# Moving a filter's second transform into the first stage and reordering the borders between batch pairs, in a long convolution followed by spectral mixing

## The chip, the core and the metric

The kernel runs on one core of one Trainium2 chip. The metric is the device time of one execution in microseconds, the median of several runs. A core has five engines with an instruction queue each: TensorE (PE, with its weight loads PEld), VectorE (DVE), ScalarE (ACT), GpSimd (POOL) and SyncE (SP). DMAs are issued here from the queues of SP and POOL. Engines meet through semaphores. Matmuls write to PSUM, of which there are eight banks; DVE and ACT read PSUM and write to SBUF ("evict").

## The reference

Two operators in a row, on `x` of 8 x 5696 x 128 (batch, sequence, channel):

```python
# 1: a causal convolution along the sequence by a filter h of 5696 x 128
L = 2 * S
Xf = np.fft.rfft(x, n=L, axis=1)
Hf = np.fft.rfft(h, n=L, axis=0)
x = np.fft.irfft(Xf * Hf[None, :, :], n=L, axis=1)[:, :S, :]
# 2: mixing of the lowest 64 modes with complex 128 x 128 weights
X = np.fft.rfft(x, axis=1)
Xr, Xi = np.real(X[:, :64]), np.imag(X[:, :64])
Y = np.zeros_like(X)
Y[:, :64] = (Xr @ w_r - Xi @ w_i) + 1j * (Xr @ w_i + Xi @ w_r)   # per mode
u = x + np.fft.irfft(Y, n=S, axis=1)
out = u + np.maximum(u @ w_ch, 0.0)
```

## The kernel before, in words

Each Fourier transform is a chain of matmuls with constant tables. A recorder (`R.add`) takes every operation in program order, adds the waits that its reads and writes need, and emits one instruction stream for each engine. So the order of the calls is the order on each engine, and most instructions of the profile carry the line of a small helper: L320 for every matmul, L308 to L314 for evictions, L317 for DMAs.

The sequence is cut as 89 x 64, and 90 frequencies `k` stand for the long axis (`NK`). They are handled in 23 groups, called ticks, of up to four frequencies (`NT = 23`, `KT = 4`; the last has two). The batch is handled in four pairs (`NP = 4`).

- **First transform**, `a_tile(j, slots, eng)` (L438), for j from 0 to 31: four matmuls of the input tile `Xin` with the table `F` into a slot of two PSUM banks, and one eviction of 128 x 720 into `As`. For j = 31 the eviction is halved: DVE takes the first bank and ACT the second ("both"). For the first pair the slots go round (0, 2, 4, 6), and `share(n)` (L428) gives an eviction to the engine with the lower load in a small table of costs, `COST`: 670 on ACT and 815 on DVE for 720 columns, 480 and 600 for 512.
- **The filter** has the same first transform earlier, which leaves `Ah`. Its second transform is `filter_tick(t, banks, eng)` (L455): 16 small matmuls of `Ah` with the table `M`, an eviction of 128 x 512 into `Hs`, two DMAs on SP's queue that copy half of the partitions to the other half, and for six of the ticks a DMA on SP's queue that loads a piece of the table `G` over the part of `Ah` that is no longer needed. `M` arrives in six pieces from POOL's queue. Six filter ticks run among the a_tiles of the first pair; the other 17 run inside the ticks of pair 0, each at the end of `tick`, six ticks ahead of its use (`LH = 6`), and DVE evicts them.
- **A tick** of a pair, `tick(g_, t)` (L612): `second(g_, t)` is the second transform (16 matmuls on `As` and `M`), `products(g_, t)` multiplies it by the filter `Hs` on DVE into `U` (usually ACT first copies PSUM into `Xs`; in a `straight` tick DVE reads PSUM itself). Two ticks later (`LC`) comes the third transform: four matmuls of `U` with `Wc`, two ACT evictions into a buffer `Zs` or `Zt`, and a DMA on SP's queue that stores it to a scratch tensor in DRAM. Three ticks later (`LM`) the matmuls with `G` add up the 64 modes in PSUM bank 7. In pairs 1 to 3 every odd tick is a `twin`: the second transform of the next tick follows in the same run of matmuls; and every fourth product is `straight`. In pair 0 there is no twin and no straight product. Pair 0 starts with six Z buffers, pairs 1 and 2 use ten.
- During a pair's ticks, the input of the next pair is loaded (POOL's queue) and placed into `Xin` by DVE copies (`x_place`).
- **The border** between two pairs: the last ticks have no second transform left, and the a_tiles of the next pair begin. Six of them stand in a table, `border`, inside the last four ticks; the 26 others follow in a loop (L696) whose slots go round (4, 6, 0, 2) after tile 6 and whose evictions alternate ACT and DVE in a fixed pattern of nine. Between the two, ACT evicts bank 7 into `XT`. After tile 31, `keep(8, 6)` issues eight matmuls that compute nothing, into banks 6 and 7. `keep` matmuls also follow the first stage (12) and the first two ticks of pair 0 (8 each). In the loop every odd tile also triggers one copy of a piece of the mixing weights on POOL's queue.
- After the four pairs come the mixing, the inverse transform of the sum and the last product (L705 to L859), which the change does not touch.

Of the kernel before, what the change touches and what calls it, by code (L numbers as in the profile page):

```python
# [123 lines left out]
def bass_long_conv_fft__then__afno_spectral_mix_kernel(nc, x, h, moe_w_r, moe_w_i, moe_w_ch, out):  # L124
# [8 lines left out]
    NP = B // 2  # L133
    KT = 4
    NT = (NK + KT - 1) // KT
# [15 lines left out]
    c, s = np.cos(th), np.sin(th)  # L151
# [75 lines left out]
    g_sb = at("G", GW, F16, a_g)  # L227
    ah_sb = at("Ah", HW, F16, a_g)
    NU, NXS, NZ, NZX = 3, 2, 6, 10
    NZS = [NZ] + [NZX] * (NP - 2) + [8]  # L230
    NZL = NZS[-1]
    a_st = take((2 * NU + NXS + NZ) * 2048)
    h_in = at("Hin", J * D, F16, a_st)
# [3 lines left out]
    XC = 4  # L237
# [214 lines left out]
             [bank(t), bank(t + 1)], [("as", j)], 1.0 / 64, eng=eng, after=once(("hp", j), HP))  # L452


    def filter_tick(t, banks, eng="vector"):  # L455
        n = len(ticks[t])
        hb = banks
        for i, k in enumerate(ticks[t]):
            for r in range(2):
                for dh in range(2):  # L460
                    mm(pv(hb[dh], i * DH, [[1, DH]]),
                       ap(m_sb, MW, J * dh, J, k * 3 * J + (J if r == 0 else 0) + dh * J, [[1, P]]),
                       ap(ah_sb, HW, J * dh, J, (2 * k + r) * DH, [[1, DH]]), r == 0, r == 1,
                       AHT + mtok(k) + [("ag", k)], [bank(hb[dh])])
        lo, hi = KT * t * D, (KT * t + n) * D
        old = once("xr", [t_ for r_ in XR for t_ in r_]) if t == 0 else []
        evac(h_sb[:, lo:hi], pv(hb[0], 0, [[DH, n], [512, 2], [1, DH]]), [bank(hb[0]), bank(hb[1])], [("h", t, 0)],
             eng=eng, after=old)
        for p0, p1 in ((0, J), (J, 0)):
            dma("sync", h_sb[p0:p0 + J, HW + lo:HW + hi], h_sb[p1:p1 + J, lo:hi], "s", [("h", t, 0)], [("h", t, 1, p0)])  # L470
        if t % 2 and t // 2 < NG:
            s0, s1 = t // 2 * GP, min(t // 2 * GP + GP, NS)
            dma("sync", g_sb[:, s0 * P:s1 * P], bass.AP(c_g, s0 * P, [[GW, P], [1, (s1 - s0) * P]]), "c", (),
                [("g", t // 2)], after=[("ag", k) for k in range(s0, s1)])
# [43 lines left out]
            [("s4", part, 0)], after=pace + (AST if part else M_ALL[1:4]))  # L518

    V, A = "vector", "scalar"  # L520
    border = {NT - 1: [(0, 0, V)], NT: [(1, 2, V), (2, 0, V)], NT + 1: [(3, 2, A), (4, 0, V)], NT + 2: [(5, 2, V)]}
    early = {0: lambda: load_id(), 1: lambda: load_w(0), 3: lambda: load_w(1), 6: lambda: load_w(2), 8: lambda: load_w(3),
             12: lambda: load_s4(1), 16: lambda: load_s4(0),
             14: lambda: clear_zt(0),
# [13 lines left out]
        for i in range(n):  # L538
            mm(pv(b0 + i % 2, 0, [[1, 2 * NK]]), f1_sb[:, 0:P], f1_sb[:, :], True, True, [("f1",)], [bank(b0 + i % 2)])

    LC, LM, LH = 2, 3, 6
    ZR = 96
    XBANKS = [bank(0), bank(1), bank(2), bank(3)]

    def with_h_at(g_, t):
        return g_ == 0 and t + LH < NT

    onchip = {}

# [5 lines left out]
        return e  # L555

    def twin(g_, t):
        return g_ > 0 and t % 2 == 1

    def straight(g_, t):  # L560
        return g_ > 0 and t % 4 == 3

    def slot_of(g_, t):
        if g_ == 0 or t == 0:
            return XSLOT[(t + 1) % 2 if t and not with_h_at(g_, t) else 0]
        return XSLOT[((t - 1) // 4 + t) % 2]

    def second(g_, t):
# [32 lines left out]
              bk + [("h", t, 0), ("h", t, 1, 0), ("h", t, 1, J)], [("u", i)])  # L601

    Z_OLD = [("ag", k) for k in range(NS, NS + 8 * (NZX - NZ))]
    XPLACE = [9, 10, 12, 15, 16, 18, 20, 22], [9, 10, 13, 14, 17, 18, 20, 22]

    def zroom(g_, s_):
        return (s_ - 2 * NZ) % NZX if g_ == 0 and s_ >= 2 * NZ else s_ % NZS[g_]

    def xtok(n):
        return [("xt", n, p_) for p_ in range(2)]  # L610

    def tick(g_, t):  # L612
        if g_ + 1 < NP:
            for i in range(2 * XC):
                if t == XPLACE[g_ > 0][i]:
                    x_place(i, x_st[i], xtok(i))
        with_h = with_h_at(g_, t)
        if t < NT:
            of_two = t > 0 and twin(g_, t - 1)
            if not of_two and not (g_ == 0 and t > LC):  # L620
                second(g_, t)
            products(g_, t, slot_of(g_, t))
            if twin(g_, t):
                second(g_, t + 1)
                if straight(g_, t):
                    copied(g_, t + 1, slot_of(g_, t + 1))
        drain = list(border[t]) if t in border and g_ + 1 < NP else []
        if drain and t >= NT:
            j, sl, e = drain.pop(0)
            a_tile(j, [sl], e)  # L630
        if g_ + 1 < NP and t % 2 == 0 and 0 < t <= 4 * XC:
            i = t // 2 - 1
            x_load(g_ + 1, i, x_st[i], xtok(i), [("u", t % NU)] + AST)
        if LC <= t < NT + LC:
            s_ = t - LC
            n = len(ticks[s_])
            i, zi = s_ % NU, zroom(g_, s_)
            zb = [turns("z", ZBANK) for b in range(2)]
            for b in range(2):
                for r in range(2):  # L640
                    mm(pv(zb[b], 0, [[1, n * D]]), (W1, W2)[r], u_s[i][:, r * 1024 + b * 512:r * 1024 + b * 512 + n * D],
                       r == 0, r == 1, [("u", i), ("wc",)] + ([("u0", i)] if s_ == 0 and b else []), [bank(zb[b])])
                evac(bass.AP(z_s[zi], b * D, [[1024, P], [2 * D, n], [1, D]]),
                     pv(zb[b], 0, [[D, n], [1, D]]), [bank(zb[b])], [("zs", zi, b)], eng="scalar",
                     after=once(("zx", zi, b), Z_OLD) if zi >= NZ else ())
            zo = (g_ * NK + KT * s_) * P * 256
            dma("sync", bass.AP(zs, zo, [[256, P], [P * 256, n], [1, 256]]),
                bass.AP(z_s[zi], 0, [[1024, P], [256, n], [1, 256]]), "z",
                [("zs", zi, 0), ("zs", zi, 1)], [("zd", g_, s_)])
            if drain and t >= NT:  # L650
                j, sl, e = drain.pop(0)
                a_tile(j, [sl], e)
        if g_ == 0 and LC <= t < NT - 1:
            second(g_, t + 1)
        if LM <= t < NT + LM:
            s_ = t - LM
            zi = zroom(g_, s_)
            for b in range(2):
                for i, k in sorted(enumerate(ticks[s_]), key=lambda q: (s_ > 0 or q[1] != 1, q)):
                    if k % 2:  # L660
                        o, off, n, sl = pv(MB, b * P, [[1, P]]), (k + 1) // 2 * P, P, (k + 1) // 2
                    else:
                        ms, off = even[k]
                        n, sl = 2 * len(ms), 0
                        dims = [[M, 2]] if len(ms) == 1 else [[ms[1] - ms[0], 2], [M, 2]]
                        o = pv(MB, b * P + ms[0], dims)
                    mm(o, z_s[zi][:, i * 256 + b * P:i * 256 + b * P + P], g_sb[:, off:off + n],
                       k == 1 and b == 0, k == NK - 1 and b == 1, [("g", sl // GP), ("zs", zi, b)], [bank(MB)])
        if drain and t < NT + LM - 1:
            j, sl, e = drain.pop(0)  # L670
            a_tile(j, [sl], e)
        if with_h:
            filter_tick(t + LH, [2, 3])

    SLOTS = [0, 2, 4, 6]
    for j in range(32):
        a_tile(j, [turns("s", SLOTS)], "both" if j == 31 else share(720))
        if j >= 11 and j % 3 == 2 and (j - 11) // 3 < LH:
            b_ = turns("s", SLOTS)
            filter_tick((j - 11) // 3, [b_, b_ + 1], share(512))  # L680
    keep(12, turns("s", SLOTS))
    for g_ in range(NP):
        for t in range(NT + LM):
            tick(g_, t)
            if g_ == 0 and t < 2:
                keep(8, 4)
            assert g_ + 1 < NP or not wp
            if g_ == NP - 1 and t in early:
                pace[:] = [("u", min(t, NT - 1) % NU)]
                early[t]()  # L690
        evac(bass.AP(xt, 2 * g_ * XTW + M, [[B * XTW, P], [XTW, 2], [1, P]]), pv(MB, 0, [[P, 2], [1, P]]),
             [bank(MB)], [("xt", g_)], 1.0 / 64, eng="scalar", after=[("ag", k) for k in range(NS + 2 * XN, NK)])
        evac(bass.AP(xt, 2 * g_ * XTW, [[B * XTW, P], [XTW, 2], [1, M]]), pv(MB, M, [[P, 2], [1, M]]),
             [bank(MB)], [("xtn", g_)], -1.0 / 64, eng="vector" if g_ + 1 == NP else "scalar", after=[("ag", k) for k in range(NS + 2 * XN, NK)])
        if g_ + 1 < NP:
            for j in range(6, 32):  # L696
                a_tile(j, [(4, 6, 0, 2)[(j - 7) % 4] if j > 6 else 0], "both" if j == 31 else (A, V)[(j - 6) % 9 % 2])
                if j == 31:
                    keep(8, 6)
                if wp and j % 2 == 1:  # L700
                    dst, src_, ring, tok = wp.pop(0)
                    dma("gpsimd", dst, src_, ring, (), [tok], after=[("as", j)])
# [189 lines left out]
```

## Time and profile before

| what | value |
|---|---|
| median of three runs | 384.91 us (384.59 to 386.44) |
| the profiled execution | 385.34 us, of it 383.2 us span |
| a_tiles of the first pair, with six filter ticks | 27.97 to 42.63 us |
| second(0) of pairs 0, 1, 2, 3 starts at | 43.88, 109.12, 164.28, 219.06 us |
| first border a_tile of pairs 1, 2, 3 | 93.03, 148.18, 202.97 us |
| Hs evictions on DVE | 22 of 128x512, 686 ns each |
| products from Xs / straight from PSUM | 69 at 1219 ns / 15 at 2284 ns (128x2048) |
| As evictions, 128x720 | ACT 64 at 784 ns, DVE 60 at 903 ns |

All times in the views are microseconds from the start of the span unless marked ns. A row of the timeline gives start, duration, engine, line, operation with its output and input tiles, their shape, and a count when several instructions are merged; in brackets stands the idle time of that engine before it, with what ended it. Rows of matmuls overlap, since they are pipelined: two of 180 columns start 0.078 us apart though each row is 0.24 us long.

### The profile page before, as it was taken

What the parts mean: (1) busy time and instruction counts of PE and PEld (TensorE: products, weight loads), DVE (VectorE), ACT (ScalarE), POOL (GpSimd) and SP (SyncE); (2) the same over time, 40 slices, a digit from 0 to 9 for tenths busy, and PEclk for the clock granted to TensorE, in tenths of its full rate; (3) what the DMA queues carried; (4) which work ended last, traced back from release to release, by engine and by line L of the source; (5) the groups of instructions that cost most, each with busy time, mean ns of one, the idle gap of its engine ahead of it and who ended that gap; (6) DMA issues with size and microseconds to landing.
All of it is one profiled execution on the core that took longest, in us unless ns stands there. A gap on an engine that the chain in (4) does not pass through costs nothing.

```text
span 383.2 us, 12588 instructions
## 1 busy us (share of the span) xinstructions
PE 366.0 (96%) x5392; PEld 283.7 (74%) x5392; DVE 310.5 (81%) x348; ACT 302.7 (79%) x488; POOL 82.5 (22%) x133
## 2 busy tenths in 40 slices
PE   7999899999989999989999999999999999999994
PEld 7998756666866666866667866668898988887873
DVE  6969888998888999998998888875447767776876
ACT  1359688898889997989997999995457676776785
POOL 8400022220552320733310411319200000000000
PEclk9999999999999999999999999997999999999999
DMA  7998469999699997999995859999999999999879
GB/s 149 194 283 339 138 125 291 273 244 261 96 138 210 226 249 220 101 133 204 263 257 164 87 167 370 334 327 388 402 402 398 414 405 406 412 405 378 359 279 356
DMA packets 86865, 103.94 MB, mean 271 GB/s; under 512 B 22638, under 2 KB 72430, under 8 KB 83330
## 3 DMA queue, kind: packets, MB, share of 16 engines
q1 hardware_dynamic: 62523, 67.73, 50.5%
q0 software_dynamic: 24288, 35.43, 44.1%
q8 instruction: 42, 0.69, 0.7%
q14 instruction: 12, 0.10, 0.1%
HBM read 70.61 MB, written 51.12 MB: 318 GB/s over the span
## 4 chain that ended last, share of the span: by engine, by line
PE 69%; ACT 10%; DMA 9%; DVE 6%; POOL 2%; issue 2%; SPq 0%; DVEq 0%; POOLq 0%
PE ps L320 69%; ACT As L310 6%; DMA Xr<-in_x_dram 4%; DMA ZT0b<-zscr 4%; POOL Xr L317 2%; DVE As L314 2%; DVE U L592 1%; ACT UT L308 1%; ACT R L826 1%; ACT Zt L308 1%; DVE Xin L356 1%; ACT Xs L308 1%; DVE U L600 1%; DVE O L827 1%; DVE UT L312 0%
## 5 line engine op out<-in xcount | busy, mean ns | idle before, releaser
L600 DVE TENSOR_TENSOR U<-Xs,Hs 128x2048 f16<-128x2048 f16 (+1 forms) x73 | 86.7, 1190 | 12.0 <-ACT Xs L308 10.4
L320 PE MATMUL ps<-U,Wc 128*128 128x512 f16 (+1 forms) x368 | 94.0, 376 | 0.0
L308 ACT CAST Xs<-ps 128x1024 f16<-128x1024 f32 (+1 forms) x77 | 75.0, 979 | 9.0 <-PE ps L320 7.4
L308 ACT CAST Zs<-ps 128x512 f16<-128x512 f32 (+1 forms) x134 | 70.6, 596 | 5.9 <-PE ps L320 5.8
L827 DVE TENSOR_TENSOR O<-ps,R 128x512 f32<-128x512 f32 x81 | 52.6, 686 | 20.5 <-ACT R L826 15.2
L826 ACT ACTIVATE R<-ps 128x512 f32<-128x512 f32 x96 | 51.0, 573 | 14.2 <-PE ps L320 13.7
L314 DVE TENSOR_SCALAR As<-ps 128x720 f16<-128x720 f32 (+1 forms) x64 | 53.2, 880 | 5.1 <-PE ps L320 3.4
L320 PE MATMUL ps<-F,Xin 128*128 128x180 f16 x512 | 52.3, 250 | 2.6 <-DVE Xin L356 1.2
L320 PE MATMUL ps<-As,M 64*128 64x128 f16 x1440 | 50.6, 217 | 4.2 <-DVE U L592 3.0
L320 PEld LDWEIGHTS ps<-As,M 64*128 64x128 f16 x1440 | 40.3, 94 | 17.9 <-issue 8.1
L310 ACT ACTIVATE As<-ps 128x720 f16<-128x720 f32 x68 | 48.0, 768 | 6.4 <-PE ps L320 5.6
L320 PE MATMUL ps<-WI,UT 128*128 128x256 f16 x360 | 52.0, 279 | 0.5 <-DVE O L827 0.4
L320 PEld LDWEIGHTS ps<-F,Xin 128*128 128x128 f16 x512 | 44.5, 155 | 9.5 <-DVE As L314 2.6
L320 PEld LDWEIGHTS ps<-U,Wc 128*128 128x128 f16 x368 | 28.7, 97 | 27.6 <-ACT Zs L308 4.4
L317 POOL DMA_DIRECT2D Xt<-in_x_dram x48 | 26.0, 545 | 104.6 <-PE ps L320 100.2
L308 ACT CAST UT<-ps 128x712 f16<-128x712 f32 x40 | 30.0, 752 | 18.8 <-PE ps L320 17.8
L320 PEld LDWEIGHTS ps<-WI,UT 128*128 128x128 f16 x360 | 39.3, 152 | 4.4 <-issue 2.1
L320 PE MATMUL ps<-IBs,C 128*128 128x356 f16 x128 | 40.1, 323 | 0.6
L320 PEld LDWEIGHTS ps<-G,Zs 128*128 128x128 f16 x524 | 27.4, 96 | 11.7
L600 DVE TENSOR_TENSOR U<-ps,Hs 128x2048 f16<-128x2048 f32 x15 | 34.3, 2284 | 0.0
L320 PE MATMUL ps<-G,Zs 128*128 128x128 f16 (+2 forms) x524 | 32.6, 192 | 0.0
L320 PE MATMUL ps<-F 128*128 128x180 f16 x280 | 27.7, 254 | 2.5 <-DMA F<-cF 2.5
(86 smaller groups left out, 506.1 us busy)
## 6 DMA issues: line engine op xcount, KB each, us to landing
out_dram<-O SPq DMA_DIRECT2D x39, 512.0 KB, 11.4
zscr<-Zs SPq DMA_DIRECT2D x64, 256.0 KB, 6.8
Xt<-in_x_dram POOLq DMA_DIRECT2D x24, 320.0 KB, 7.0
zscr<-Zt SPq DMA_DIRECT2D x24, 256.0 KB, 6.6
W<-wscr POOLq DMA_DIRECT2D x4, 1024.0 KB, 8.9
M<-cM POOLq DMA_DIRECT2D x5, 720.0 KB, 20.5
ZT0a<-zscr SPq DMA_DIRECT2D x3, 1024.0 KB, 14.0
Hs<-Hs SPq DMA_DIRECT2D x44, 64.0 KB, 5.8
```

The source lines that it names most:

```text
L308: R.add(e, lambda h_: h_.copy(dst, src), reads, writes, after=after)
L310: R.add(e, lambda h_: h_.activation(dst, src, COPY, scale=scale), reads, writes, after=after)
L314: R.add(e, lambda h_: h_.tensor_scalar_mul(dst, src, scale), reads, writes, after=after)
L317: R.add(eng, lambda h_: h_.dma_start(dst, src), reads, writes, ring=ring, after=after)
L320: R.add("tensor", lambda h_: h_.matmul(o, l, r, start=st, stop=sp), reads, writes)
L356: R.add("vector", lambda e: e.tensor_copy(bass.AP(x_sb, i * XN * XS, [[XW, NQ], [XS, XN], [1, D]]), bass.AP(src, 0, [[XB, NQ], [D, XN], [1 ...
L592: R.add("vector", lambda e, b=b, s_=s_: e.tensor_tensor(bass.AP(u_s[i], b * 512, [[2048, P], [1024, 2], [1, n * D]]), s_, hv, MULT), [tok, ...
L600: R.add("vector", lambda e: e.tensor_tensor(uv, src, hv, MULT), bk + [("h", t, 0), ("h", t, 1, 0), ("h", t, 1, J)], [("u", i)])
L826: R.add("scalar", lambda e: e.activation(rv, src_r, RELU), bk, [("r", i % NR)], after=once(("r", i % NR), G_ALL + XTT + [("y", 0), ("y", 1 ...
L827: R.add("vector", lambda e: e.tensor_tensor(ov, src_u, rv, ADD), bk + [("r", i % NR)], [key + (h_,)], after=once(key, old))
```

## The change: what it does

- All 23 filter ticks now stand in the first stage. After a_tile(j), as many are issued as `due` says: two each time, from j = 5 on, the last after j = 30. Each takes the next slot and an engine by `share(512)`. The loop over the ticks of pair 0 has none.
- Pair 0 uses the same order as the others: twins, straight products, ten Z buffers, one list of ticks for `x_place`, and no special slots. `LH`, `with_h_at` and the keep matmuls of its first two ticks go; `keep(12, ...)` becomes `keep(8, ...)`.
- `tick` is split: its third transform becomes `third(g_, s_)`, its modes `modes_of(g_, s_)`.
- The border is written out in place of the table: for the first three pairs the ticks end at 22, and then follow third(21), tiles 0 and 1, third(22), tile 2, modes_of(20), tile 3, modes_of(21), tile 4, modes_of(22), the XT evictions, and the loop from tile 5, with slots (0, 4, 6, 2). `share` chooses the engine everywhere, with loads set at the border.

```diff
-    NZS = [NZ] + [NZX] * (NP - 2) + [8]
+    NZS = [NZX] * (NP - 1) + [8]
...
     def twin(g_, t):
-        return g_ > 0 and t % 2 == 1
+        return t % 2 == 1
 
     def straight(g_, t):
-        return g_ > 0 and t % 4 == 3
+        return t % 4 == 3
...
-    def tick(g_, t):
...
-        drain = list(border[t]) if t in border and g_ + 1 < NP else []
-        if drain and t >= NT:
-            j, sl, e = drain.pop(0)
-            a_tile(j, [sl], e)
...
+    def third(g_, s_):
+        if 0 <= s_ < NT:
...
+    def modes_of(g_, s_):
+        if 0 <= s_ < NT:
...
-        if with_h:
-            filter_tick(t + LH, [2, 3])
+
+    def tick(g_, t):
+        if g_ + 1 < NP:
+            for i in range(2 * XC):
+                if t == XPLACE[i]:
+                    x_place(i, x_st[i], xtok(i))
+        if t < NT:
+            of_two = t > 0 and twin(g_, t - 1)
+            if not of_two:
+                second(g_, t)
+            products(g_, t, slot_of(g_, t))
+            if twin(g_, t):
+                second(g_, t + 1)
+                if straight(g_, t):
+                    copied(g_, t + 1, slot_of(g_, t + 1))
+        if g_ + 1 < NP and t % 2 == 0 and 0 < t <= 4 * XC:
+            i = t // 2 - 1
+            x_load(g_ + 1, i, x_st[i], xtok(i), [("u", t % NU)] + AST)
+        third(g_, t - LC)
+        modes_of(g_, t - LM)
 
     SLOTS = [0, 2, 4, 6]
+    done = 0
     for j in range(32):
         a_tile(j, [turns("s", SLOTS)], "both" if j == 31 else share(720))
-        if j >= 11 and j % 3 == 2 and (j - 11) // 3 < LH:
+        due = NT if j == 30 else max(0, j - 2) * NT // 28 // 2 * 2
+        while done < due:
             b_ = turns("s", SLOTS)
-            filter_tick((j - 11) // 3, [b_, b_ + 1], share(512))
-    keep(12, turns("s", SLOTS))
+            filter_tick(done, [b_, b_ + 1], share(512))
+            done += 1
+    keep(8, turns("s", SLOTS))
     for g_ in range(NP):
-        for t in range(NT + LM):
+        for t in range(NT + LM if g_ + 1 == NP else NT):
             tick(g_, t)
-            if g_ == 0 and t < 2:
-                keep(8, 4)
...
+        if g_ + 1 < NP:
+            load.update(scalar=600.0, vector=0.0)
+            third(g_, NT - 2)
+            a_tile(0, [0], share(720))
+            a_tile(1, [2], share(720))
+            third(g_, NT - 1)
+            load["scalar"] += 560.0
+            a_tile(2, [0], share(720))
+            modes_of(g_, NT - 3)
+            a_tile(3, [4], share(720))
+            modes_of(g_, NT - 2)
+            a_tile(4, [2], share(720))
+            modes_of(g_, NT - 1)
+            load["scalar"] += 700.0
...
         if g_ + 1 < NP:
-            for j in range(6, 32):
-                a_tile(j, [(4, 6, 0, 2)[(j - 7) % 4] if j > 6 else 0], "both" if j == 31 else (A, V)[(j - 6) % 9 % 2])
+            for j in range(5, 32):
+                a_tile(j, [(0, 4, 6, 2)[(j - 5) % 4]], "both" if j == 31 else share(720))
                 if j == 31:
                     keep(8, 6)
```

More of the change, by code (lines that the diff above doesn't have):

```diff
@@ L452, in a_tile, with filter_tick @@
              [bank(t), bank(t + 1)], [("as", j)], 1.0 / 64, eng=eng, after=once(("hp", j), HP))
-    def filter_tick(t, banks, eng="vector"):
+    def filter_tick(t, banks, eng):
         n = len(ticks[t])
@@ L520, in bass_long_conv_fft__then__afno_spectral_mix_kernel @@
     V, A = "vector", "scalar"
-    border = {NT - 1: [(0, 0, V)], NT: [(1, 2, V), (2, 0, V)], NT + 1: [(3, 2, A), (4, 0, V)], NT + 2: [(5, 2, V)]}
     early = {0: lambda: load_id(), 1: lambda: load_w(0), 3: lambda: load_w(1), 6: lambda: load_w(2), 8: lambda: load_w(3),
@@ L539, in keep @@
             mm(pv(b0 + i % 2, 0, [[1, 2 * NK]]), f1_sb[:, 0:P], f1_sb[:, :], True, True, [("f1",)], [bank(b0 + i % 2)])
-    LC, LM, LH = 2, 3, 6
+    LC, LM = 2, 3
     ZR = 96
     XBANKS = [bank(0), bank(1), bank(2), bank(3)]
-    def with_h_at(g_, t):
-        return g_ == 0 and t + LH < NT
     onchip = {}
@@ L557, in twin @@
     def twin(g_, t):
-        return g_ > 0 and t % 2 == 1
+        return t % 2 == 1
     def straight(g_, t):
-        return g_ > 0 and t % 4 == 3
+        return t % 4 == 3
     def slot_of(g_, t):
-        if g_ == 0 or t == 0:
-            return XSLOT[(t + 1) % 2 if t and not with_h_at(g_, t) else 0]
+        if t == 0:
+            return XSLOT[0]
         return XSLOT[((t - 1) // 4 + t) % 2]
@@ L603, in bass_long_conv_fft__then__afno_spectral_mix_kernel @@
     Z_OLD = [("ag", k) for k in range(NS, NS + 8 * (NZX - NZ))]
-    XPLACE = [9, 10, 12, 15, 16, 18, 20, 22], [9, 10, 13, 14, 17, 18, 20, 22]
+    XPLACE = [9, 10, 13, 14, 17, 18, 20, 22]
     def zroom(g_, s_):
-        return (s_ - 2 * NZ) % NZX if g_ == 0 and s_ >= 2 * NZ else s_ % NZS[g_]
+        return s_ % NZS[g_]
     def xtok(n):
         return [("xt", n, p_) for p_ in range(2)]
-    def tick(g_, t):
[L613 to L626, printed above, removed]
-        drain = list(border[t]) if t in border and g_ + 1 < NP else []
-        if drain and t >= NT:
-            j, sl, e = drain.pop(0)
-            a_tile(j, [sl], e)
[L631 to L635, printed above, removed]
+    def third(g_, s_):
+        if 0 <= s_ < NT:
             n = len(ticks[s_])
@@ L649, in tick @@
                 [("zs", zi, 0), ("zs", zi, 1)], [("zd", g_, s_)])
[L650 to L656, printed above, removed]
+    def modes_of(g_, s_):
+        if 0 <= s_ < NT:
             zi = zroom(g_, s_)
@@ L668, in tick @@
                        k == 1 and b == 0, k == NK - 1 and b == 1, [("g", sl // GP), ("zs", zi, b)], [bank(MB)])
-        if drain and t < NT + LM - 1:
-            j, sl, e = drain.pop(0)
-            a_tile(j, [sl], e)
-        if with_h:
-            filter_tick(t + LH, [2, 3])
+    def tick(g_, t):
[17 more added lines that the diff above has]
+        modes_of(g_, t - LM)
     SLOTS = [0, 2, 4, 6]
+    done = 0
     for j in range(32):
         a_tile(j, [turns("s", SLOTS)], "both" if j == 31 else share(720))
-        if j >= 11 and j % 3 == 2 and (j - 11) // 3 < LH:
+        due = NT if j == 30 else max(0, j - 2) * NT // 28 // 2 * 2
+        while done < due:
             b_ = turns("s", SLOTS)
-            filter_tick((j - 11) // 3, [b_, b_ + 1], share(512))
-    keep(12, turns("s", SLOTS))
+            filter_tick(done, [b_, b_ + 1], share(512))
+            done += 1
+    keep(8, turns("s", SLOTS))
     for g_ in range(NP):
-        for t in range(NT + LM):
+        for t in range(NT + LM if g_ + 1 == NP else NT):
             tick(g_, t)
-            if g_ == 0 and t < 2:
-                keep(8, 4)
             assert g_ + 1 < NP or not wp
```

## The prediction

> **What bounds the kernel now.** I read four views in this order: the page, the sums of each engine by stage, the timeline of two stages, and the DMA issues. From the page:
>
> ```profile
> span 383.2 us, 12588 instructions
> PE 366.0 (96%) x5392; PEld 283.7 (74%) x5392; DVE 310.5 (81%) x348; ACT 302.7 (79%) x488; POOL 82.5 (22%) x133
> PE 69%; ACT 10%; DMA 9%; DVE 6%; POOL 2%; issue 2%; SPq 0%; DVEq 0%; POOLq 0%
> ```
>
> The second line is busy time, the third the shares of the chain that ended last. TensorE carries 69% of that chain, yet the 96% says little, because a matmul's row is longer than its step. So I cut the span where a stage begins: the first a_tile at 27.97, and second(0) of pairs 0 to 3.
>
> ```profile
> core 0: us, PE busy (x) PEld busy (x) DVE busy (x) ACT busy (x) POOL busy (x), PEclk, DMA share, GB/s
> 27.97:43.88 15.91, 15.76 (x236) 13.77 (x237) 14.58 (x19) 14.54 (x20) 0.00 (x0) 1.00 0.78 284
> 43.88:109.12 65.24, 63.34 (x1048) 42.72 (x1050) 56.48 (x66) 55.88 (x87) 17.41 (x28) 1.00 0.93 203
> 109.12:164.28 55.16, 53.10 (x768) 37.74 (x769) 50.98 (x49) 50.81 (x82) 17.17 (x29) 1.00 1.02 193
> 164.28:219.06 54.78, 52.82 (x769) 37.73 (x770) 50.99 (x49) 50.80 (x82) 15.53 (x26) 1.00 0.97 190
> ```
>
> Pair 0 with its border takes 65.24 us, pairs 1 and 2 take 55.16 and 54.78. Pair 0 alone has filter ticks inside it, and an order of its own. Now the first stage, in the timeline of PE and DVE:
>
> ```profile
> 34.16 0.41 PE L320 MATMUL ps<-Ah,M 64*128 64x64 f16 x16
> 34.50 1.27 PE L320 MATMUL ps<-F,Xin 128*128 128x180 f16 x12
> 34.78 0.68 DVE L312 CAST Hs<-ps 128x512 f16<-128x512 f32 x1
> 35.50 0.91 DVE L314 TENSOR_SCALAR As<-ps 128x720 f16<-128x720 f32 x1
> 35.71 0.41 PE L320 MATMUL ps<-Ah,M 64*128 64x64 f16 x16
> ```
>
> Columns are start, duration, engine, line, operation. One filter tick and three a_tiles, which are four slots of PSUM, return every 1.55 us, or 0.39 per item. A filter tick holds PE 0.34 us (34.16 to 34.50).
>
> **The change, part by part.**
>
> *First stage.* 17 of the 23 filter ticks move here, so 38 items become 55. The 38 ran from 27.97 to 42.63, where the keep matmuls start: 14.66 us, 0.386 an item. Upper price: 17 x 0.386 = 6.6 us, if four slots in rotation go on setting the pace. Middle: 17 x 0.34 = 5.8 if PE does. Lower: share() now gives some filter evictions to ACT, and no row of the trace has ACT evicting Hs. The nearest is ACT's Zs from 128x512, 0.606 us alone and two in 1.08, so 0.48 apart; DVE's Hs takes 0.686. Both engines together make one in 1/(1/0.48 + 1/0.686) = 0.28, or 4.8 us. New assignments by the cost table: ACT 16 a_tiles and 14 filter ticks, DVE 15 and 9, one a_tile halved. At the spacing of their rows (ACT 0.69 and 0.48 to 0.61, DVE 0.82 and 0.69) either engine has 18 to 20 us, and PE 32 x 0.375 + 23 x 0.34 = 19.8, so all three are full together and the rotation rules. I take **+6.2**, near the rotation.
>
> *Waits behind it.* The last piece of M is issued at 13.3 and lands 25.7 later, at 39.0; the first filter tick to need it is about the 47th item, at 27.97 + 46 x 0.386 = 45.7. Cost nothing, with 6.7 us of cover. The 46 Hs copies and 6 G loads of the filter now all stand on SP's queue before pair 0's first store of Zs. At 0.55 an Hs issue and up to 1.0 a G they run from about 32 to 32 + 25.3 + 6 = 63, while the first store is wanted at about 54. Stores wait there, and who waits for them is the eviction that reuses a Zs buffer. Ten buffers now serve pair 0, so it is tick 10's: pair 1's first store comes 4.6 us after its second(0), a tick takes 1.7, so 50.1 + 4.2 + 17 = 71.3. A store lands 6.8 us after issue, at 70. Cost nothing, with a cover of 1.5 us only; without it see the first rival. The ticks' own need of Hs comes later still.
>
> *Pair 0's ticks.* Without filter work, with the order of the other pairs (two ticks of second() together, every fourth product straight from PSUM), I price pair 0 at what pairs 1 and 2 show: 65.24 - 55.0 = **-10.3**. Of it 17 x 0.34 = 5.8 is PE's filter work and 16 x 0.078 = 1.2 the keep matmuls of ticks 0 and 1; the rest is ACT's copies, five fewer, and the gaps between shorter runs of matmuls. The first stage's four dropped keep matmuls count nothing: they end before the eviction that second(0) waits for. The x loads are issued at the same ticks as pair 1's.
>
> *Borders, three times.* At the start, from the timeline of PE:
>
> ```profile
> 148.18 0.85 PE L320 MATMUL ps<-F,Xin 128*128 128x180 f16 x8 [0.38 <-DVE Xin L356]
> 152.89 1.16 PE L320 MATMUL ps<-F,Xin 128*128 128x180 f16 x12 [0.16 <-DVE As L314]
> 154.29 9.05 PE L320 MATMUL ps<-F,Xin 128*128 128x180 f16 x92 [0.25 <-ACT As L310]
> ```
>
> third(21) ahead of a_tile(0) fills the 0.38 us wait for Xin. But a_tile(2) then needs slot 0 back from a_tile(0): the eviction ends near 150.0 by DVE's 0.90, while PE is done at 149.6. And a_tile(7) needs banks 6 and 7, so the XT evictions, which come after the same modes_of as before. Walking the new order with these rows I get a_tile(9)'s eviction at 154.8, against 154.87. From there to 30 both orders give ACT 12 and DVE 10 tiles. Gain 0.1. The end:
>
> ```profile
> 162.36 1.87 ACT L310 ACTIVATE As<-ps 128x720 f16<-128x720 f32 x3
> 162.67 1.36 DVE L314 TENSOR_SCALAR As<-ps 128x720 f16<-128x720 f32 x2
> 163.20 0.79 PE L320 MATMUL ps<-F 128*128 128x180 f16 x8
> 164.28 1.07 PE L320 MATMUL ps<-As,M 64*128 64x128 f16 x32 [0.29 <-ACT As L310]
> ```
>
> Eight keep matmuls run at 163.20, while the two halves of a_tile(31) are evicted until 164.23; then second(0) starts. They write banks 6 and 7, and tile 31 sat in slot 4. In the new order j = 31 takes slot 6, the very banks. The keep matmuls then wait for both halves, and second(0) stands behind them: 8 x 0.078 = 0.6 later. Each border **+0.5**, three times **+1.5**. Bounds: all three waits above gone (0.79) and 0.6 paid, -0.2 each; or nothing gained and a quarter more for a restart, +0.8 each. The weight copies on POOL, 14 in a border where 13 were, have nothing behind them that is due: 0.
>
> **Sum:** +6.2 - 10.3 + 1.5 = -2.6. The profiled execution took 385.34 (its span of 383.2 and 2.1 around it), so 382.7; the median of the runs is 0.43 below that execution, so I forecast **382.3**.
>
> **The rivals.** *SP's queue becomes the bound (slower).* Place: pair 0's tick 12, where ACT's Zs eviction waits for the store of tick 0. For it:
>
> ```profile
> 73.16 0.59 SPq L317 DMA_DIRECT2D zscr<-Zs x1
> 73.85 1.63 SPq L317 DMA_DIRECT2D Hs<-Hs x2
> Hs<-Hs SPq DMA_DIRECT2D x44, 64.0 KB, 5.8
> ```
>
> With x loads and stores under way two Hs issues took 1.63, 0.8 each, not 0.55. 46 x 0.77 + 6 = 41.4 brings the first store to 73.4, landed at 80.2, 8.9 late: 382.3 + 8.9 = 391.2. It decides once an Hs issue averages over 0.58. Against it: in this stage few other transfers run until pair 0's tick 2. Chance 0.15. *The moved work hides (faster).* First stage +4.8, borders -0.2 each: -6.1, 378.8. For it: evictions now split over two engines. Against: the 0.39 pace in both patterns of the stage. Chance 0.17. *The move is worth nothing.* Pairs of filter ticks hold two slots at once, items take 0.5 us: +8.5, borders +0.8 each: -10.3 + 8.5 + 2.4 = +0.6, 385.5. A tile waiting 0.12 for its slot at 34.92 hints at it. Chance 0.07. *The clock drops.* The granted clock shows 0.50 once, over some 6.8 us from 263, where the small matmuls of the mixing run; that is 3.4 us lost at most. Were the dropped keep matmuls of pair 0 to bring the same once more: 382.3 + 3.4 = 385.7. Against: pairs 1 and 2 start without any, with PE waiting 0.87 us, at clock 1.00. Chance 0.06. The Trainium skill ("TensorE: Matmul & The Clock Gate", part 1 on the HAM clock gate) has the clock halve after an idle window of about 3.4 us; by that rule no wait of this change is long enough, but the trace's own drop came without such a wait, so the rule does not settle it.
>
> **How the numbers follow.** Forecast 0.55, with a range of its own of 380.9 to 384.0 (first stage 4.8 to 7.2, borders 0.9 to 2.1). No change means within 0.5%, 1.9 us, about what repeated runs of this kernel can tell: 383.0 to 386.8. The forecast falls below 383.0 three times in four, 0.41; with the hidden move 0.58 for faster. Same: 0.14 + 0.07 + 0.06 less a little that drifts over, 0.25. Slower 0.17. The range 379.0 to 386.2 leaves out the slower rival and part of the faster.
>
> **What would show it.** Right: second(0) of pair 0 near 50.1; the three pairs near 55.5 each; the eight matmuls ps<-F at a border after, not beside, the last As evictions, and second(0) right behind; products straight from PSUM 20 instead of 15; first Zs store near 62 with no ACT wait at tick 12. Wrong: a first stage longer than 23.5 us or shorter than 20.5, ACT waiting for DMA in pair 0, borders shorter than 16 us, or a second stretch of half clock.

## The result, and the profile after

The changed kernel takes 390.25 us (median of four runs, 388.88 to 393.12) against 384.87 for the kernel before (its three runs and a fourth): a ratio of 1.013, 95% interval 1.010 to 1.016. It is slower, by 5.4 us, where 382.3 was forecast. The profiled execution took 391.2 us, its span 389.1. Medians in this text are of all runs; ratios and their intervals leave out one slow run each of e2, e3, e7 and e9 below, over 1.5% longer than the fastest of its kernel.

The sums by stage of the kernel after, cut at the same events as before (first a_tile, then second(0) of pairs 0 to 3):

```profile
core 0: us, PE busy (x) PEld busy (x) DVE busy (x) ACT busy (x) POOL busy (x), PEclk, DMA share, GB/s
27.94:49.82 21.88, 21.27 (x496) 18.06 (x497) 19.26 (x25) 19.18 (x31) 0.00 (x0) 1.00 0.78 267
49.82:113.94 64.12, 55.61 (x768) 38.78 (x770) 50.34 (x48) 51.34 (x83) 18.22 (x30) 0.95 0.95 192
113.94:168.98 55.04, 53.00 (x769) 37.63 (x768) 50.17 (x48) 51.27 (x83) 18.18 (x30) 1.00 1.04 196
168.98:224.06 55.08, 53.01 (x769) 37.62 (x769) 50.18 (x48) 51.32 (x83) 12.87 (x23) 1.00 0.90 183
```

second(0) of pair 0 starts 5.94 us later, at 49.82 instead of 43.88, as planned. Pairs 1 and 2 are where they were (-0.12 and +0.30). But pair 0, which now holds the same instructions as pair 1, takes 64.12 us and not 55: only 1.12 less than before. Its PE was busy 55.61, and its granted clock was 0.95. What follows pair 2 is 0.90 longer. Together +5.9, the difference of the spans.

The chain that ended last, from 69 us on, shows where pair 0 stood still (start, duration, what):

```profile
69.40 0.62 ACT Zt L308 x2
70.02 8.05 DMA zscr<-Zs
78.07 0.02 issue
...
78.15 0.59 ACT Zs L308
```

An eviction into `Zs` waits for a store from that buffer, which was issued only at 70.02. The timelines of SP's queue, ACT and PE show the cause and the effect:

```profile
31.33 2.44 SPq L317 DMA_DIRECT2D Hs<-Hs  x4
...
53.30 16.68 SPq L317 DMA_DIRECT2D Hs<-Hs  x22
70.02 8.08 SPq L317 DMA_DIRECT2D zscr<-Zs  x6
```

```profile
78.15 1.07 ACT L308 CAST Zs<-ps 128x512 f16<-128x512 f32 x2 [7.77 <-DMA zscr<-Zs]
```

```profile
71.81 0.60 PE L320 MATMUL ps<-U,Wc 128*128 128x512 f16 x2
78.79 1.03 PE L320 MATMUL ps<-U,Wc 128*128 128x512 f16 x2 [6.38 <-ACT Zs L308]
```

The first store of pair 0 stands behind all 46 Hs copies and 6 G loads. They took SP from 31.33 to 70.02. The store landed at 78.07, and tick 10's eviction, which reuses the buffer of tick 0, had waited 7.77 us for it; PE stood 6.38 us. One more thing came with it: while PE stood, the clock fell to half,

```profile
77.00:78.00 1.00, 0.00 (x0) 0.00 (x0) 0.00 (x0) 0.00 (x0) 0.00 (x0) 0.58 1.03 234
78.00:80.00 2.00, 1.21 (x8) 0.67 (x9) 0.00 (x0) 1.85 (x3) 0.00 (x0) 0.50 1.06 273
```

(the third number from the end is the clock), and it came back near 84. Of the 9.08 us that pair 0 takes more than pair 1, 6.4 are the wait. The remainder of 2.7 fits the half clock: PE works from 78.79 to about 84 at half speed, 5.2 us for 2.6 us of work, and its busy time in pair 0 is 2.6 above that in pair 1 (55.61 against 53.00). This is the first rival of the prediction, with its place and its cause; how much of its time was luck is told below.

The border of the changed kernel, from the timeline of PE before second(0) of pair 2:

```profile
156.41 11.02 PE L320 MATMUL ps<-F,Xin 128*128 128x180 f16 x108
168.15 0.90 PE L320 MATMUL ps<-F 128*128 128x180 f16 x8 [0.72 <-DVE As L314]
168.98 1.07 PE L320 MATMUL ps<-As,M 64*128 64x128 f16 x32
```

The eight keep matmuls now come after PE has waited for tile 31's eviction, and second(0) follows right behind them. Before, they ran inside that wait.

### The profile page after: what moved, and what is told of

The parts are those of the page before. It is cut to its first block, busy times and chain, and to the rows that moved or that the text cites. A ratio compares the mean times of both kernels' runs of the same rounds, so it can differ in the third digit from the quotient of the medians.

```text
span 389.1 us, 12544 instructions
## 1 busy us (share of the span) xinstructions
PE 363.9 (94%) x5372; PEld 283.3 (73%) x5372; DVE 305.7 (79%) x334; ACT 303.8 (78%) x497; POOL 81.8 (21%) x133
## 4 chain that ended last, share of the span: by engine, by line
PE 72%; DMA 11%; DVE 7%; ACT 6%; POOL 2%; issue 1%; SPq 0%; DVEq 0%; ACTq 0%; POOLq 0%
PE ps L320 71%; DMA ZT0b<-zscr 4%; DMA Xr<-in_x_dram 4%; DVE As L314 4%; DMA zscr<-Zs 2%; POOL Xr L317 2%; DVE U L588 1%; ACT R L826 1%; ACT As L310 1%; ACT UT L308 1%; ACT Zt L308 1%; ACT Xs L308 1%; DMA Hs<-Hs 1%; DVE UT L312 0%; SPq L317 0%
## 5 line engine op out<-in xcount | busy, mean ns | idle before, releaser
L320 PE MATMUL ps<-U,Wc 128*128 128x512 f16 (+1 forms) x368 | 96.0, 380 | 6.4 <-ACT Zs L308 6.4
L596 DVE TENSOR_TENSOR U<-Xs,Hs 128x2048 f16<-128x2048 f16 (+1 forms) x68 | 80.6, 1188 | 19.5 <-ACT Xs L308 17.2
L308 ACT CAST Xs<-ps 128x1024 f16<-128x1024 f32 (+1 forms) x72 | 69.5, 971 | 9.7 <-PE ps L320 7.6
L308 ACT CAST Zs<-ps 128x512 f16<-128x512 f32 (+1 forms) x126 | 66.0, 603 | 8.1 <-DMA zscr<-Zs 8.1
L314 DVE TENSOR_SCALAR As<-ps 128x720 f16<-128x720 f32 x64 | 53.5, 880 | 7.6 <-PE ps L320 6.2
L310 ACT ACTIVATE As<-ps 128x720 f16<-128x720 f32 (+1 forms) x68 | 48.9, 771 | 9.0 <-PE ps L320 7.9
L320 PE MATMUL ps<-As,M 64*128 64x128 f16 x1440 | 49.2, 218 | 3.7 <-DVE U L588 3.5
L596 DVE TENSOR_TENSOR U<-ps,Hs 128x2048 f16<-128x2048 f32 x20 | 45.7, 2283 | 0.0
L308 ACT CAST Zt<-ps 128x512 f16<-128x512 f32 (+1 forms) x58 | 30.9, 603 | 0.0
L320 PE MATMUL ps<-G,Zs 128*128 128x2 f16 (+2 forms) x492 | 30.9, 193 | 0.0
```

The costliest lines, as they stand in the source:

```text
L308: R.add(e, lambda h_: h_.copy(dst, src), reads, writes, after=after)
L310: R.add(e, lambda h_: h_.activation(dst, src, COPY, scale=scale), reads, writes, after=after)
L314: R.add(e, lambda h_: h_.tensor_scalar_mul(dst, src, scale), reads, writes, after=after)
L320: R.add("tensor", lambda h_: h_.matmul(o, l, r, start=st, stop=sp), reads, writes)
L596: R.add("vector", lambda e: e.tensor_tensor(uv, src, hv, MULT), bk + [("h", t, 0), ("h", t, 1, 0), ("h", t, 1, J)], [("u", i)])
```

## The experiments

Each is compared with runs of the kernel before beside it on the same chip; their median was 385.89 us for e1 to e4, 386.51 for e5, e6, e7 and e9, and 385.48 for e10. The edits are against the changed kernel, shortened where "..." stands, and the comments in them are this text's. `h_copy(t)` issues the Hs copies that `filter_tick` issued before.

**Stores of pair 0 on another queue** (e1):

```diff
-            dma("sync", bass.AP(zs, zo, ...), ..., "z", ...)
+            dma("gpsimd" if g_ == 0 else "sync", bass.AP(zs, zo, ...), ..., "g" if g_ == 0 else "z", ...)
```

> Pair 0's 23 stores of Zs and Zt are issued on POOL's queue instead of SP's; the number of transfers and their order of need stay. Theory (the stores stand behind 46 Hs copies and 6 G loads on SP's queue): the first store is issued near 54 instead of 70, ACT no longer waits 7.8 us for a store, the half-clock stretch near 77 goes with it, and pair 0 takes 55 to 56 us as pairs 1 and 2 do: about 381 us, ratio to the kernel before 0.99. Rival (the DMA engines are full in this stretch, and stores land 8 to 10 us late from any queue): ACT still waits 4 us or more, 386 us or above.

Measured: 382.04 us, ratio 0.992 (0.989 to 0.994). By its sums by stage pair 0 takes 8 us less than in the changed kernel, at full clock (the second line is pair 1):

```profile
50.08:106.22 56.14, 53.47 (x768) 37.85 (x769) 50.69 (x48) 51.61 (x83) 36.65 (x53) 1.00 0.92 217
106.22:161.37 55.15, 53.07 (x770) 37.75 (x770) 50.26 (x48) 51.34 (x83) 18.69 (x31) 1.00 1.06 197
```

The first store is issued at 56.5, behind an x load on POOL's queue, and no eviction waits for one, though the stores take 8.0 us to land in the median and up to 9.5. So it was the place in SP's queue, not the engines of the DMA: Hs copies (until 73.3), x loads and stores still run side by side.

**More places in the ring of Hs copies** (e3): 

```diff
-    for name, n in (..., ("s", 8), ...):
+    for name, n in (..., ("s", 24), ...):
```

> The ring of semaphores for Hs copies has 24 places instead of 8, nothing else. If waits of a copy for the one eight places ahead hold SP back (2.3 us seen at 63.6 to 65.9, about 3.4 in all), the first store comes near 66.6 instead of 70 and ACT's wait falls from 7.8 to about 4.4: 385 to 387 us. If the issue time of a copy on SP alone rules, the first store stays within 1 us of 70 and the time near 390.

Measured: 385.78 us, ratio 1.001 (0.999 to 1.003). The first store comes at 68.5, 1.5 earlier, not 3.4; ACT's longest waits are

```profile
74.41 1.07 ACT L308 CAST Zs<-ps 128x512 f16<-128x512 f32 x2 [3.55 <-DMA zscr<-Zs]
...
79.25 1.07 ACT L308 CAST Zs<-ps 128x512 f16<-128x512 f32 x2 [0.95 <-DMA zscr<-Zs]
```

instead of 7.77. So copies waiting for the one eight places ahead were a small part of the delay on SP: 0.74 us a copy become 0.71. The rest is the issue of 52 DMAs one by one. Even so the kernel is 4.5 us shorter. The first store also lands in 5.8 us here and in 8.05 there, so that it is there 3.7 us earlier, and the clock is halved for about 3.4 us instead of 6.8. Why it lands sooner was not tested.

**Copies of ticks 6 to 22 issued in pair 0's ticks**, each behind a store (e2):

```diff
+        if t < HL:                      # in filter_tick, HL = 6
+            h_copy(t)
...
+        if g_ == 0 and t + HL < NT:     # at the end of tick
+            h_copy(t + HL)
```

> All filter matmuls and evictions stay in the first stage, but the Hs copies of ticks 6 to 22 are issued in pair 0's ticks, six ticks ahead, behind each tick's store. Theory: stores are on time, pair 0 takes 55 to 56 us, about 381 us. Rival (pair 0 is slow because its copies, stores and x loads share the engines): the same bytes at the same time as in the kernel before, pair 0 stays at 60 us or above.

Measured: 386.66 us, ratio 1.002 (1.000 to 1.005). The stores are on time and no eviction waits, but pair 0 takes 59.59 us: the products now wait, four times, 4.2 us in all. Timeline of DVE, two of the four, then of SP:

```profile
73.23 1.23 DVE L603 TENSOR_TENSOR U<-Xs,Hs 128x2048 f16<-128x2048 f16 x1 [1.52 <-DMA Hs<-Hs]
...
87.70 2.29 DVE L603 TENSOR_TENSOR U<-ps,Hs 128x2048 f16<-128x2048 f32 x1 [1.08 <-DMA Hs<-Hs]
```

```profile
61.75 1.62 SPq L317 DMA_DIRECT2D Hs<-Hs  x2
63.42 0.60 SPq L317 DMA_DIRECT2D zscr<-Zs  x1
```

Two copies and a store take 1.6 + 0.6 = 2.2 us of SP, and a tick of pair 0 now takes 1.7. The expectation missed this: in the kernel before a tick lasted 2.29 us, which SP could just follow. The same queue binds, by its rate instead of its backlog: from 59.7 to 87 its rows follow each other almost without a gap.

**Half as many copies** (e4), one for two filter ticks, the same bytes:

```diff
-        for p0, p1 in ((0, J), (J, 0)):
-            dma("sync", h_sb[p0:p0 + J, HW + lo:HW + hi], h_sb[p1:p1 + J, lo:hi], ...)
+        if t % 2 or t == NT - 1:
+            t0 = t // 2 * 2
+            lo = KT * t0 * D
+            for p0, p1 in ((0, J), (J, 0)):
+                dma("sync", h_sb[p0:p0 + J, HW + lo:HW + hi], h_sb[p1:p1 + J, lo:hi], "s", ...)
```

> One Hs copy for two filter ticks: 24 copies of up to 128 KB in place of 46 of 64 KB, the same bytes. Theory (a count of issues on SP): 22 copies fewer at 0.75 us each bring the first store 16 us forward, to about 54, where it is wanted; no ACT wait for a store; pair 0 55 to 56 us; about 381 us. Rival (bytes rule, not issues): the first store still after 62 and a wait of ACT remains.

Measured: 385.38 us, ratio 1.000 (0.997 to 1.002). Pair 0 does what was expected: 55.15 us, no wait for a store, with the stores back on SP. The last twelve copies, from the timeline of SP:

```profile
45.52 10.11 SPq L317 DMA_DIRECT2D Hs<-Hs  x12
```

That is 0.84 us for a copy of up to 128 KB, where the last 22 copies of up to 64 KB in the changed kernel took 0.76 each (16.68 us). So the number of issues is what matters far more than the bytes. But second(0) of pair 0 starts at 53.74 instead of 50: something new in the first stage, below.

**Copies by two, the later ones spread** (e7): ticks 0 to 11 in the first stage, 12 to 22 in pair 0, two copies for every second tick.

```diff
+        if t < HL and t % 2:                        # in filter_tick, HL = 12
+            h_copy(t - 1)                           # ticks t - 1 and t at once
...
+        if g_ == 0 and t + HL < NT and t % 2 == 0:  # at the end of tick
+            h_copy(t + HL)
```

> Stores stay on SP. One Hs copy for two ticks, those of ticks 0 to 11 in the first stage, those of 12 to 22 spread over pair 0, two for every second tick. SP then has about one copy and one store in a tick, 0.7 + 0.6 = 1.3 us against a tick of 1.7. Theory (issue time of SP's queue): no wait for a store nor for a copy, pair 0 55 to 56 us, and with second(0) at 50 as in e1 the time is within 0.7 us of e1's 382.0. Rival (only another queue helps): pair 0 above 57.

Measured: 385.32 us, ratio 0.997 (0.994 to 1.000). Pair 0 takes 55.16 us, so SP can serve both if it has fewer issues there; but second(0) is again late, at 53.19. The time is missed by 3 us, all of it in the first stage.

**The first stage's wait.** In e4, e7 and e9 (below) PE stops at one point for 2.2 to 2.5 us (2.48, 2.20 and 2.38) and waits for nothing that the profile shows, and the clock is halved behind it; in the kernels with single copies there (the changed one, e1, e2, e3, e5, e6) PE waits 0.3 us at most at this point, at full clock. e10 has single copies in the first stage (ticks 0 to 11) and copies by two only in pair 0, with the keep matmuls moved as in e5 below:

```diff
+        if t < HL:                                  # in filter_tick, HL = 12
+            h_copy(t)                               # tick t alone
...
+        if g_ == 0 and t + HL < NT and t % 2 == 0:  # at the end of tick
+            h_copy(t + HL)                          # ticks t + HL and the next
```

> Stores on SP, keep matmuls in banks 2 and 3. In the first stage one Hs copy for each tick (ticks 0 to 11, 64 KB each, as in e1), in pair 0 one for two ticks (12 to 22). e4, e7 and e9 have the doubled copies in the first stage and there a wait of PE of 2.4 to 2.7 us near 42 that the profile gives to nothing, with the clock halved behind it; e1, e5 and e6 have single copies and neither. If the doubled copies in the first stage bring it, it is gone: second(0) of pair 0 near 50, pair 0 near 54.8, total 380.2 as e5. If it comes with the moving of copies into pair 0's ticks or with the doubled ones as such, second(0) is again at 53 to 54 and the time near e9's 383.9.

Measured: 379.55 us, ratio 0.984 (0.977 to 0.990), the lowest median of all, though its ratio is the same as e5's below. second(0) starts at 50.08, pair 0 takes 54.48. At the same place in PE's stream, timeline of e9 and then of e10:

```profile
44.21 0.46 PE L320 MATMUL ps<-F,Xin 128*128 128x180 f16 x2 [2.38 <-issue]
```

```profile
42.24 0.32 PE L320 MATMUL ps<-F,Xin 128*128 128x180 f16 x2 [0.24 <-issue]
```

and the sums of the stretch before it, for e9 with the stretch of the stop, and then for e10:

```profile
38.00:42.00 4.00, 3.83 (x90) 3.21 (x89) 3.43 (x6) 3.70 (x7) 0.00 (x0) 1.00 1.03 260
42.00:46.00 4.00, 1.79 (x37) 1.47 (x37) 1.31 (x2) 1.09 (x2) 0.00 (x0) 0.67 0.96 242
```

```profile
38.00:42.00 4.00, 4.00 (x90) 3.38 (x91) 3.42 (x6) 3.87 (x7) 0.00 (x0) 1.00 0.69 211
```

With doubled copies there the DMA engines are full up to 42 (1.03 against 0.69, the last but one column; 1.01 to 1.03 in all three kernels that stop, 0.67 to 0.73 in all that don't). The one packet that the instruction queue (q8) moves near this point runs at 39.6 in e10 and at 41.4 in e9, and in both, as in e4 and e7, PE goes on 2.5 to 2.8 us after it. That the doubled copies in the first stage bring the wait is shown; that PE waits for its own instructions, late behind full engines, fits the records but was not tested.

**The border.** e5 is e1 with one digit changed, so that the keep matmuls write banks that were free long before:

```diff
-                    keep(8, 6)
+                    keep(8, 2)
```

> e1 (stores of pair 0 on POOL) with one digit more: the border's eight keep matmuls write banks 2 and 3 instead of 6 and 7, where tile 31 sits. My border step says that they cost 0.65 us in front of second(0) at each of three borders: pairs 0 to 2 each 0.6 to 0.7 shorter than in e1 (54.4 to 54.5 for pairs 1 and 2), total 1.9 below e1, about 380.1. Rival (second(0) waits for the last As eviction in any case and the matmuls cost nothing): same as e1.

Measured: 380.17 us, ratio 0.984 (0.979 to 0.989), 1.9 below e1, or 2.5 when each is taken from the kernel before beside it. Timeline of PE and the sums of pairs 1 and 2:

```profile
157.94 0.79 PE L320 MATMUL ps<-F 128*128 128x180 f16 x8
159.02 1.07 PE L320 MATMUL ps<-As,M 64*128 64x128 f16 x32 [0.28 <-ACT As L310]
```

```profile
104.61:159.02 54.41, 52.81 (x769) 37.59 (x770) 50.20 (x48) 51.30 (x83) 18.78 (x31) 1.00 1.06 198
159.02:213.43 54.41, 52.83 (x769) 37.60 (x770) 50.26 (x48) 51.30 (x83) 13.15 (x23) 1.00 0.94 188
```

The matmuls are inside the wait again, and pairs 1 and 2 are 0.74 and 0.65 shorter than in e1. Pair 0 is 1.33 shorter: 0.69 of it at its border, from the first border tile on (15.30 us against 15.99), the rest in the ticks before, where nothing was changed and the cause is open. e9 is e7 with the same digit:

> e7 with the keep matmuls in banks 2 and 3. If both steps hold: 1.9 us below e7, about 380.1, the fastest with e5. If the keep matmuls cost nothing: as e7.

Measured: 383.92 us, 1.4 below e7, ratio 0.992 (0.990 to 0.995); pairs 0 to 2 take 54.4 to 54.5. The step at the border holds, the forecast of 380.1 does not: the wait in the first stage is there as in e7, and the half clock behind it lasts longer (until 50.2 instead of 47.9), so second(0) starts at 54.20, another 1.0 us later. e6 is e1 with the old border:

```diff
-        for t in range(NT + LM if g_ + 1 == NP else NT):
+        for t in range(NT + LM):
...
-            for j in range(5, 32):
-                a_tile(j, [(0, 4, 6, 2)[(j - 5) % 4]], "both" if j == 31 else share(720))
+            for j in range(6, 32):
+                a_tile(j, [(4, 6, 0, 2)[(j - 7) % 4] if j > 6 else 0], "both" if j == 31 else (A, V)[(j - 6) % 9 % 2])
```

> e1 with the kernel before's border: its table of six tiles, its slots, its fixed pattern of engines. If the new order of the border gains about what its keep matmuls cost, pairs 1 and 2 stay within 0.3 of e1's 55.1 and the time within 1 us of e1's 382.0. If my sum was right (new border +0.5 each), it is 1.5 us faster than e1, 380.5. If the new border is a gain of its own, over 383.

Measured: 381.69 us, ratio 0.988 (0.982 to 0.993), within noise of e1. Its pairs 1 and 2 take 54.78 and 54.91, e1's 55.15 and 55.06, e5's 54.41. So at these two borders the new order by itself gains about 0.4 us (e6 less e5), and the banks of its keep matmuls cost about 0.7 (e1 less e5).

## Why the prediction was wrong, point by point

**The failed step** is the term of "Waits behind it" for the stores: the first store was to be issued at 63 and land at 70, "Cost nothing, with a cover of 1.5 us only". The price of an Hs issue was too low. It takes SP 0.74 us on average (46 copies in 38.7 us less 0.8 for each of six G loads), and not 0.55, which was the lowest of the rows, not their mean. In the kernel before, on SP:

```profile
51.71 1.13 SPq L317 DMA_DIRECT2D Hs<-Hs  x2
...
61.80 2.27 SPq L317 DMA_DIRECT2D Hs<-Hs  x2
```

Its 15 rows of two copies in pair 0 add up to 22.95 us, 0.77 a copy; only the one above and the one at 53.86 come to 0.56. At 0.74 the 46 copies make the first store 8.6 us later than forecast; an earlier start and cheaper G loads take back 1.9, so it was issued at 70.02. It landed in 8.05 us and not 6.8 (five stores and four x loads were issued between 69.3 and 73.4, which would fit; it was not tested), and it was wanted at 70.4 and not 71.3. By the terms of the prediction itself the cover was 1.2 us (71.3 less 63.3 and 6.8). Together the store came 7.7 us late. The assumption "few other transfers run until pair 0's tick 2" was false on both sides: the last pieces of M were still arriving until about 40, and the x loads of tick 2 begin at 55.2, with 18 of the 46 copies still to come. A cover of 1.5 us behind 25.3 us of copies needed an accuracy of 6% in the price of an issue, and the chance of 0.15 did not say that.

**The rival** was right in place and mechanism, and its price of an issue, 0.77, is the mean of those 15 rows. That its total came so near (391.2, measured 390.25, and 391.2 in the profiled execution) is in part luck: it let the store land 8.9 us late and counted all of that as time. The store came 7.7 late, PE stood 6.4, and 2.7 came from the half clock, which its sum did not hold. The half clock, held to be a rival of its own with a chance of 0.06, was part of that loss; it came because PE stood, not because keep matmuls were dropped: e1 drops the same ones, and pair 0 runs at full clock.

**First stage**, +6.2: right in size (5.94; second(0) at 49.82 against "near 50.1", and at 49.80 to 50.34 in the six experiments without the wait). That lies between PE's price of 5.8 and the rotation's of 6.6; which of them sets the pace was not tested.

**Pair 0's ticks**, -10.3: right in mechanism, hidden by the stall. With the stores out of the way and the border still that of the change, pair 0 takes 56.14 (e1) or 55.15 (e4), -9.1 and -10.1 against 65.24.

**Borders**, +1.5: the sign is right and the size is not. The cost of the keep matmuls was right (0.65 to 0.74 measured, 0.6 forecast). The gain of the new order was forecast as 0.1 and is about 0.4. So a border costs 0.15 to 0.37 (e1 against e6, pairs 1 and 2) and not 0.5.

**The forecast as a whole** is near what e1 shows, where only the stall is taken away: 382.04 against 382.3. Part of that is luck too. Pair 0 with its border takes 0.6 more than forecast (56.14 against 55.5) and pairs 1 and 2 take 0.7 less, and the kernel before was 1.0 us slower beside e1 than in the runs of the forecast.

## What to carry to other kernels

When work is moved ahead, its DMAs move ahead too, and they take their places in front of whatever the same queue was to issue next: count the issues of the whole queue up to the first transfer that someone needs, at their mean price in the trace (here 0.77 us in pair 0 of the kernel before) and not at the lowest row (0.56). A cover that is small against the sum in front of it is no cover. Matmuls that only fill a wait must write banks that are free before the wait begins; in the banks that are waited for they become part of it, here for about 0.7 us a border. Both are mended in e10 by halving the number of copies where they meet the stores and by one digit at the border: 379.55 us, 1.6% faster than the kernel before (interval 1.0 to 2.3%).

## What was not expected of the hardware

- The clock fell to half after shorter pauses of PE than thought: in e3 PE was idle for 2.16 us before 75.06, and the granted clock of the stretch from 75 to 76 was 0.59, of the next 0.50. The Trainium skill ("TensorE: Matmul & The Clock Gate", part 1 on the HAM clock gate) names an idle window of about 3.4 us; here less was enough, as behind the stops of 2.2 to 2.5 us in e4, e7 and e9, and the measurement decides.
- A PE stream can stop for 2.2 to 2.5 us with no semaphore in sight (e4, e7, e9), at the same matmul each time, when the DMA engines were full before it (a share of 1.01 to 1.03 from 38 to 42 us). The cause was not tested.
- The stretch after the pairs differs by up to 1.4 us between kernels that are the same there (163.6 in e10, 165.0 in the kernel after); what sets it was not tested.
